# New place shifts, by operation name and by pair of heads, in the order of a fused attention, FFN and routed-expert kernel

## The chip, the cores and the metric

The kernel runs on one core of a Trainium2 chip. The time is device microseconds of one execution; the kernel before has a median of 493.71 us over three runs (492.6 to 497.37). The profile is of one further execution, with its own time.

## The reference, cut to what matters

Three layers are computed in a row on 1152 tokens (batch 2, sequence 576, model width 512 = 8 heads of 64): causal attention with a bias from a running sum, a dense feed-forward layer, and a layer of 8 experts of which each token takes one.

```python
# attention: q, k, v of 2 x 8 x 576 x 64
scores = scale * np.matmul(q, k.transpose(0, 1, 3, 2))
cum = np.cumsum(np.maximum(s, 0.0), axis=-1)
bias = -(cum[:, :, :, None] - cum[:, :, None, :])
scores = np.where(causal, -1000000000.0, scores + np.minimum(bias, 0.0))
attn = np.exp(scores - np.max(scores, axis=-1, keepdims=True))
attn = attn / (np.sum(attn, axis=-1, keepdims=True) + 1e-09)
x = np.matmul(attn, v)                      # to 1152 x 512
# dense layer: 512 -> 2048 -> 512
h = x @ w_in
x = (h * (1.0 / (1.0 + np.exp(-1.702 * h)))) @ w_out
# experts: argmax of 8 logits, at most 288 tokens each, 512 -> 1024 -> 512
expert_idx = np.argmax(x @ w_gate, axis=1)
y = np.maximum(disp @ w1, 0.0) @ w2         # disp: the tokens, gathered by expert
out[i] = gate_w[i] * y[expert_idx[i], pos[i]]
```

## The kernel before

**Attention** works on 8 pairs of heads, numbered 0 to 7. A pair has 5 row blocks t = 0 to 4 of 64, 128, 128, 128 and 128 rows. For one block, `unit` makes the scores on PE (L719, and the mask by L720) in the banks SC, takes the maximum on DVE (L741 or L745), the exponent on ACT (L750, tile pexp), casts it to 16 bits on DVE (L704, tile ph) and adds the low part on POOL (L764, L769). SP then issues a DMA transpose PT<-ph (L777; blocks 0 and 1 share the tile PT01, the others are PT2, PT3 and PT4). `av_unit` multiplies PT with the values V on PE (L797), scales on DVE (L809 to L812, tile xs) and transposes the result on PE (L821).

What a pair needs first: SP loads k and q (L667, tiles kraw and qraw, two of each), PE transposes them (L688), ACT or DVE copies them into the tile QK (L694, L697; QK0 and QK1 in turn), and SP adds two rows with the bias from a tensor cum_d in DRAM (L677, QK<-cum_d). The tensor cum_d is written once, at the start, by two DMAs (L542). Values are loaded by SP (L594, into spare tiles named vraw, th2, woL7 and wiL7 at the start) and split by ACT (L655) and DVE (L657) into V.

**The dense layer** loads its weights in pieces of 512 KB (L358, L361, tiles wraw0 to wraw2), converts them on ACT, DVE and POOL (L392 to L409) and multiplies in `mm1` (L433, L437) and `mm2` (L466, L467); part of this fills the gaps of the attention. **Routing** (about 335 to 347 us) computes logits, the ranks and the order of tokens; the first expert's tokens are gathered by PE (L1007 makes the selection on DVE, L1010 multiplies) and split into a high and a low part by `xs_first` (ACT L1306, L1312; DVE L1308, L1315). **Experts:** per expert `e_mm1` (L1372, L1374; DVE L1380 and L1384 behind it), `e_mm2` (L1401, L1403; DVE L1410) and stores; DVE also splits expert weights (L1295).

**What sets the order.** Every operation is put into the class `Plan` with a rank, its place. `Plan.run` makes a list schedule: on each engine, of the operations that it believes ready within 120 ns, the one with the lowest rank goes next. The instructions are then issued in that order; each engine runs its own in order, SP's DMA issues too. `SHIFT` is a table from a name to a number that is added to the rank. The name is made of the stage (a, b0 to b4 by row block, or c), the functions, the engine and the tile. So one number holds for, say, all transposes PT<-ph of row block 3 in all pairs.

Of the kernel before, what the change touches and what calls it, by code (L numbers as in the profile page):

```python
# [22 lines left out]
SHIFT = {  # L23
    "a.bias_keep.sp.cumd": 3.9, "a.bias_rows.sp.QKb": -7.7, "a.consts.a.pool.identF": -19.5, "a.consts.b.pool.": 13.3,
    "a.consts.dve.identB": -28.5, "a.consts.dve.ones1": 13.2, "a.consts.dve.ph": 22.6, "a.consts.dve.vss": 9.9,
    "a.consts.pool.QKb": 1.4, "a.consts.pool.V2o": 22.6, "a.prologue.dve.cum": 6.7, "a.prologue.dve.neg": 5.3,
    "a.prologue.dve.one": 16.1, "a.prologue.dve.one2": 25.2, "a.prologue.dve.s": 22, "a.prologue.sp.s": -32.6,
    "a.qk_T.act.QK": 9.4, "a.qk_T.dve.QK": -10.1, "a.qk_T.tr.pe.BK": 13.3, "a.qk_load.sp.raw": -15.6,
    "a.v_load.sp.vraw": 14.3, "a.v_scale.dve.gtb": 34.4, "a.v_scale.dve.scl": 37.3, "a.v_scale.pe.BK": 16.3,
# [1581 lines left out]
```

## Time and profile before

| | |
|---|---|
| median of 3 runs | 493.71 us |
| the profiled execution's own time | 495.86 us |
| its span in the trace | 494.1 us |
| PE busy | 465.5 us, 94% |
| DVE, ACT, POOL busy | 359.3, 328.6, 128.4 us |
| mean granted clock of PE | 0.979 |

The page gives the span in 40 slices of 12.35 us each, with the granted clock of TensorE in tenths; 1.0 is 2.4 GHz and 0.5 is 1.2 GHz. In a row of the timeline a bracket at the end gives how long the engine stood idle before the row and what the trace takes as the releaser. In a row of a table by stretches each engine has its busy time and, in brackets, its instructions.

### The profile page before, as it was taken

The numbers are of one execution on the slowest core, as the hardware profiler recorded it, in microseconds if no ns is written. First come the engines' busy times: TensorE is split into PE (matmuls) and PEld (weight loads), VectorE is DVE, ScalarE is ACT, GpSimd is POOL, SyncE is SP. The second block draws the span as 40 slices with busy tenths as digits, with TensorE's granted clock in tenths as the row PEclk, the third lists the DMA queues.
The fourth block names the chain that finished last, engine by engine and source line by source line (L and its number), as shares of the span: only waits on it lengthen the run. The fifth ranks groups of instructions, "written<-read, shape, count | busy, mean of one in ns | idle before, by whom it ended". The sixth has DMA issues, their size and how long they took to land.

```text
span 494.1 us, 9648 instructions
## 1 busy us (share of the span) xinstructions
PE 465.5 (94%) x3379; PEld 352.1 (71%) x3398; DVE 359.3 (73%) x817; ACT 328.6 (67%) x754; POOL 128.4 (26%) x136
## 2 busy tenths in 40 slices
PE   6599989999999999999999999999999999989993
PEld 5366666667677666766766966759688898878981
DVE  8867767888979988982324466846986879799980
ACT  3567878987557656673335346842886988899981
POOL 5616765867212222211000130002000110220250
PEclk9968989999999999999999999999999999999998
DMA  7997999978972554692000248821694687876820
GB/s 164 255 226 150 239 233 171 211 148 152 206 217 96 172 155 148 215 356 87 1 1 0 87 172 312 323 84 44 195 348 151 184 265 243 288 241 226 273 84 21
DMA packets 99047, 88.20 MB, mean 179 GB/s; under 512 B 66679, under 2 KB 77943, under 8 KB 98982
## 3 DMA queue, kind: packets, MB, share of 16 engines
q1 hardware_dynamic: 97108, 82.04, 61.3%
q0 software_dynamic: 1888, 5.52, 2.9%
q8 instruction: 27, 0.44, 0.4%
q14 instruction: 24, 0.20, 0.1%
HBM read 60.60 MB, written 14.19 MB: 151 GB/s over the span
## 4 chain that ended last, share of the span: by engine, by line
PE 49%; DMA 13%; DVE 12%; issue 10%; ACT 8%; POOL 5%; SPq 1%; POOLq 0%; DVEq 0%; ACTq 0%
PE SC L466 8%; PE SC L719 6%; PE MI L433 5%; DMA PT<-ph 5%; PE MX L433 4%; DMA out_dram<-x2R,small 4%; PE SC L467 3%; PE MI L437 2%; PE AV L1401 2%; PE AV L797 2%; PE MX L437 2%; DMA wraw<-in_moe_w_out_dram 2%; POOL ph L769 2%; PE MI L1372 2%; POOL ph L764 2%
## 5 line engine op out<-in xcount | busy, mean ns | idle before, releaser
L466 PE MATMUL SC<-woH,gtH 128*128 128x512 f32 x212 | 75.8, 481 | 0.0
L719 PE MATMUL SC<-QK 128*128 128x512 f32 (+4 forms) x192 | 65.1, 449 | 8.5 <-POOL ph L769 4.3
L447 DVE SCALAR_TENSOR_TENSOR gtH<-th,gtH 128x384 fp32r<-128x384 f32 x46 | 25.8, 561 | 40.0 <-ACT gtH L445 39.3
L764 POOL TENSOR_TENSOR ph<-pexp,ph 128x512 f16<-128x512 f32 (+4 forms) x32 | 44.7, 1398 | 31.8 <-DVE ph L704 26.3
L450 ACT ACTIVATE gtB<-th 128x384 bf16<-128x384 f32 x46 | 24.0, 521 | 37.1 <-PE SC L467 24.5
L433 PE MATMUL MI<-xT,wiH 128*128 128x384 f32 x216 | 47.0, 356 | 0.5 <-DVE th L443 0.4
L750 ACT ACTIVATE pexp<-SC,smA 128x192 f32<-128x192 f32 (+4 forms) x80 | 38.4, 520 | 12.7 <-DVE smA L741 9.2
L719 PEld LDWEIGHTS SC<-QK 128*128 128x128 f32 (+1 forms) x192 | 29.8, 197 | 23.1 <-issue 11.4
L466 PEld LDWEIGHTS SC<-woH,gtH 128*128 128x128 f32 x212 | 40.3, 194 | 3.2
L1295 DVE TENSOR_TENSOR wiL<-wraw,wiH 128x1024 bf16<-128x1024 f32 x32 | 38.9, 1221 | 3.7 <-ACT wiH L1294 3.5
L1295 DVE TENSOR_TENSOR woL<-wraw,woH 128x1024 bf16<-128x1024 f32 x32 | 38.9, 1218 | 3.1 <-ACT woH L1294 3.0
L1437 POOL DMA_INDIRECT out_dram<-x2R,small x8 | 9.9, 1240 | 119.1 <-ACT x2R L1464 82.5
L409 POOL TENSOR_TENSOR wiL<-wvi,wiH 128x512 bf16<-128x512 f32 x16 | 22.2, 1386 | 68.6 <-ACT wiH L405 64.2
L467 PEld LDWEIGHTS <-gtB 128*128 128x128 bf16 x138 | 13.2, 96 | 37.5 <-issue 37.2
L433 PEld LDWEIGHTS MI<-xT,wiH 128*128 128x128 f32 x216 | 37.8, 189 | 2.2 <-DVE th L443 0.9
L1118 POOL DMA_INDIRECT xs_d<-x2R,small x9 | 9.0, 996 | 112.9 <-DVE small L1058 57.3
L433 PE MATMUL MX<-xT,wiH 128*128 128x384 f32 x168 | 36.6, 358 | 0.1
L467 PE MATMUL SC<-woL,gtB 128*128 128x512 bf16 x94 | 36.7, 390 | 0.0
L1294 ACT ACTIVATE wiH<-wraw 128x1024 fp32r<-128x1024 f32 x32 | 33.6, 1055 | 1.9 <-DMA wraw<-in_moe_w_dram 1.4
L694 ACT ACTIVATE QK<-MI 64x288 f32<-64x288 f32 x57 | 24.1, 423 | 14.6 <-PE MI L688 9.0
L1294 ACT ACTIVATE woH<-wraw 128x1024 fp32r<-128x1024 f32 x32 | 33.5, 1055 | 0.4 <-DMA wraw<-in_moe_w_dram 0.4
L433 PEld LDWEIGHTS MX<-xT,wiH 128*128 128x128 f32 x168 | 29.6, 189 | 1.6 <-DVE th L443 0.8
(290 smaller groups left out, 1146.3 us busy)
## 6 DMA issues: line engine op xcount, KB each, us to landing
wraw<-in_moe_w_dram SPq DMA_DIRECT2D x64, 512.0 KB
wraw<-in_moe_w_in_dram SPq DMA_DIRECT2D x16, 512.0 KB
wraw<-in_moe_w_out_dram SPq DMA_DIRECT2D x16, 512.0 KB
xs_d<-x2R SPq DMA_DIRECT2D x16, 257.0 KB
kraw<-in_k_dram SPq DMA_DIRECT2D x8, 288.0 KB
qraw<-in_q_dram SPq DMA_DIRECT2D x8, 288.0 KB
out_dram<-x2R SPq DMA_DIRECT2D x9, 256.0 KB
x2R<-xs_d SPq DMA_DIRECT2D x8, 257.0 KB
```

What stands on the lines that cost most here:

```text
L409: e_.tensor_tensor(out=dlo, in0=vi.bitcast(F32), in1=dhi.bitcast(F32), op=ALU.subtract)
L433: nc.tensor.matmul(ps, lhsT=whi[:, kc], rhs=xT[:, a, kc, cs], start=(kc == 0 and a == 0), stop=False)
L447: pl.op("dve", t_dve(CN), lambda: nc.vector.scalar_tensor_tensor(out=gh[:, 1], in0=th, scalar=0.5, in1=gh[:, 0].bitcast(F32), op0=ALU.mult ...
L450: pl.op("act", t_act(CN), lambda: nc.scalar.activation(out=gb, in_=th, func=AF.Copy, scale=0.5), r=[("th", n % 2)], w=[("gtb", gi)] + xw)
L466: nc.tensor.matmul(o, lhsT=gh[:, a, ts], rhs=whi, start=(fc == 0 and a == 0), stop=False)
L467: nc.tensor.matmul(o, lhsT=gb[:, ts], rhs=wlo, start=False, stop=(fc == NFC - 1))
L694: pl.op("act", t_act(3 * TQ, False) + 130, lambda o=o, in_=in_, sc=sc: nc.scalar.activation(out=o, in_=in_, func=AF.Copy, scale=sc), r=[bk ...
L719: nc.tensor.matmul(o[:rows, j0:j1], lhsT=t_[:, 2 * r, i0:i0 + rows], rhs=t_[:, 2 * r + 1, j0:j1], start=True, stop=False)
L750: pl.op("act", t_act(wdt, False, 1), lambda o=o, r=r, nm=nm: nc.scalar.activation(out=pe[:rows, r, :wdt], in_=o[:rows, :wdt], func=AF.Exp, ...
L764: pl.op(eng, (t_pool if eng == "pool" else t_dve)(n * T_), lambda rs_=rs_, e_=e_: e_.tensor_tensor(out=hl[:, rs_, 0:T_], in0=pe[:rows, rs_ ...
L1294: pl.op("act", t_act(1024), lambda: nc.scalar.activation(out=dhi, in_=raw, func=AF.Copy), r=[rk], w=kh, rank=rank, after=after)
L1295: pl.op("dve", t_dve(1024), lambda: nc.vector.tensor_tensor(out=dlo, in0=raw, in1=dhi.bitcast(F32), op=ALU.subtract), r=[rk, ks[0], ks[2]] ...
```

## The change

All numbers of the table are new, and there are about 320 entries for about 205. Beside an entry for a name there may now be a second one for the name and a group: `@` in stage a, `@n` for the pair n of heads in stage b (`@x` behind the attention), `@n` for the n-th dozen of ranks in stage c. The operations themselves, 860 up to the order of tokens and 1773 in all that follows or overlaps, are the same.

```diff
 SHIFT = {
-    "a.bias_keep.sp.cumd": 3.9, "a.bias_rows.sp.QKb": -7.7, "a.consts.a.pool.identF": -19.5, ...
...
-        rank += SHIFT.get(self.name(eng, fn, w, rank), 0.0)
+        name = self.name(eng, fn, w, rank)
+        rank += SHIFT.get(name, 0.0) + SHIFT.get(name + self.group(name, rank), 0.0)
...
+    def group(self, name, rank):
+
+        return {"a": "@", "b": f"@{int(rank // 5)}" if rank < 40.0 else "@x", "c": f"@{int(rank // 12)}"}[name[0]]
```

The lines of the changed kernel are higher by 37 below the table (L677 is L714 there, L777 is L814).

**First place: the start, SP.** SP's issues from the V loads into spare tiles to the first transposes, before:

```order
L594 DMA th2_88<-in_v_dram 128x8x64
L594 DMA woL7_85<-in_v_dram 128x8x64
L594 DMA wiL7_81<-in_v_dram 128x8x64
L667 DMA kraw1_116<-in_k_dram 96x2x384
L667 DMA qraw1_114<-in_q_dram 96x2x384
L542 DMA cum_d_72<-QK1_112 8x2x1152 x2
L667 DMA kraw0_115<-in_k_dram 96x2x384
L667 DMA qraw0_113<-in_q_dram 96x2x384
L358 DMA wraw0_91<-in_moe_w_in_dram 128x4x256
L777 DMA_TRANSPOSE PT01_123<-ph01_122 128x8x128
L358 DMA wraw2_93<-in_moe_w_in_dram 128x4x256
```

The next issue there is `L677 DMA QK1_112<-cum_d_72`. The same stretch of the changed kernel, from the first write of cum_d on:

```order
L579 DMA cum_d_72<-QK1_112 8x2x1152 x2
L631 DMA th2_88<-in_v_dram 128x8x64
L631 DMA woL7_85<-in_v_dram 128x8x64
L631 DMA wiL7_81<-in_v_dram 128x8x64
L704 DMA kraw1_116<-in_k_dram 96x2x384
L704 DMA qraw1_114<-in_q_dram 96x2x384
L714 DMA QK1_112<-cum_d_72 2x2304
L395 DMA wraw0_91<-in_moe_w_in_dram 128x4x256
L395 DMA wraw2_93<-in_moe_w_in_dram 128x4x256
L814 DMA_TRANSPOSE PT01_123<-ph01_122 128x8x128
L704 DMA kraw0_115<-in_k_dram 96x2x384
```

The writes of cum_d went ahead of three V loads, and QK1<-cum_d went ahead of the two weight loads, the transpose PT01 and the loads of pair 2 (kraw0, qraw0). PT01 now stands behind wraw2.

On PE, in the kernel before, the rows around the first matmuls on QK1 with what each waits for (DMAHW4 is the semaphore of the transfer QK1<-cum_d there):

```order
L688 MATMUL MI_109<-identF_60,qraw1_114 128x96 [waits DMAHW4_49,Activation_49]
L688 MATMUL MI_109<-identF_60,qraw1_114 128x96 x2
L719 MATMUL SC1_106<-QK1_112 128x192 [waits DMAHW4_49,Activation_49,Pool_49]
L688 MATMUL MI_109<-identF_60,qraw1_114 128x96 x3
L719 MATMUL SC0_105<-QK1_112 64x64
L719 MATMUL SC1_106<-QK1_112 128x192 [waits Activation_49]
```

In the changed kernel the block of 64 rows goes first here, and its first matmul has the same kind of waits.

**Second place: pair 2, SP.** The issues between the transposes PT2 and PT4 of pair 2, before:

```order
L777 DMA_TRANSPOSE PT2_127<-ph2_124 128x10x128
L667 DMA qraw1_114<-in_q_dram 96x2x384
L594 DMA th2_88<-in_v_dram 128x8x64
L667 DMA kraw0_115<-in_k_dram 96x2x384
L677 DMA QK0_111<-cum_d_72 2x2304
L777 DMA_TRANSPOSE PT3_128<-ph3_125 128x14x128
L594 DMA woL7_85<-in_v_dram 128x8x64
L777 DMA_TRANSPOSE PT4_129<-ph4_126 128x18x128
```

And in the changed kernel:

```order
L814 DMA_TRANSPOSE PT2_127<-ph2_124 128x10x128
L631 DMA th2_88<-in_v_dram 128x8x64
L814 DMA_TRANSPOSE PT3_128<-ph3_125 128x14x128
L631 DMA woL7_85<-in_v_dram 128x8x64
L704 DMA qraw1_114<-in_q_dram 96x2x384
L714 DMA QK0_111<-cum_d_72 2x2304
L704 DMA kraw0_115<-in_k_dram 96x2x384
L814 DMA_TRANSPOSE PT4_129<-ph4_126 128x18x128
```

PT3 passed the loads of q and k and the bias rows; PT4 still stands behind them all.

**Third place: the end of routing, DVE.** The rows around `xs_first` (gtH is the high part of the first expert's tokens in four pieces, srt, sqr and ordi belong to the order of tokens), before:

```order
L1164 TENSOR_TENSOR sqr<-srt,iota_66 128x64
L1308 TENSOR_TENSOR gtH<-MI,gtH 128x224
L1165 TENSOR_TENSOR sqr<-sqr,iota_66 128x64
L1166 TENSOR_REDUCE srt_1961<-sqr 128x8
L1308 TENSOR_TENSOR gtH<-MX,gtH 128x224
L1308 TENSOR_TENSOR gtH<-SC_105,gtH 128x224
L1315 CAST gtB<-gtH 128x224
L1167 CAST ordi<-srt_1961 128x8
L1172 TENSOR_TENSOR sqr<-iota_66,srt 128x64
L1308 TENSOR_TENSOR gtH<-SC_105,gtH 128x224
```

And in the changed kernel:

```order
L1202 TENSOR_TENSOR sqr<-sqr,iota_66 128x64
L1203 TENSOR_REDUCE srt_1961<-sqr 128x8
L1345 TENSOR_TENSOR gtH<-MI,gtH 128x224
L1204 CAST ordi<-srt_1961 128x8
L1209 TENSOR_TENSOR sqr<-iota_66,srt 128x64
L1345 TENSOR_TENSOR gtH<-MX,gtH 128x224
L1345 TENSOR_TENSOR gtH<-SC_105,gtH 128x224
L1352 CAST gtB<-gtH 128x224
L1210 TENSOR_TENSOR sqr<-sqr,misc 128x64
L1211 TENSOR_REDUCE misc<-sqr 128x8
L1345 TENSOR_TENSOR gtH<-SC_105,gtH 128x224
```

Four small operations of the token order moved ahead of a piece of gtH that they stood behind: two ahead of the first piece (L1202, L1203) and two ahead of the last (L1210, L1211).

## Rows read from the trace of the kernel before

**Rows 1.** The page: span, PE's busy time, PE's granted clock in slices

```profile
span 494.1 us, 9648 instructions
PE 465.5 (94%) x3379; PEld 352.1 (71%) x3398; DVE 359.3 (73%) x817; ACT 328.6 (67%) x754; POOL 128.4 (26%) x136
PEclk9968989999999999999999999999999999999998
```

**Rows 2.** Table by stretches: length, busy us, granted clock, DMA share, GB/s

```profile
12.35:24.70 12.35, 6.88 (x36) 3.78 (x34) 10.87 (x23) 7.08 (x14) 8.60 (x8) 0.92 1.12 255
24.70:37.00 12.30, 11.96 (x90) 8.18 (x91) 7.90 (x16) 7.91 (x19) 2.29 (x3) 0.67 1.09 227
37.00:49.40 12.40, 11.77 (x111) 8.48 (x110) 9.34 (x21) 9.92 (x24) 7.73 (x9) 0.86 0.77 150
61.80:74.10 12.30, 10.19 (x114) 7.57 (x113) 8.24 (x18) 9.25 (x23) 7.80 (x7) 0.86 1.20 234
148.00:345.00 197.00, 196.50 (x1057) 141.09 (x1071) 125.26 (x302) 105.13 (x204) 25.10 (x21) 1.00 0.42 142
```

**Rows 3.** Timeline of PE, 11 to 35 us: start, duration, operation, idle before

```profile
11.61 0.81 PE L719 MATMUL SC<-QK 128*128 128x320 f32 x2 [0.92 <-ACT pexp L750]
...
24.68 0.98 PE L719 MATMUL SC<-QK 128*128 128x192 f32 x2 [4.32 <-POOL ph L769]
...
29.36 0.97 PE L797 MATMUL AV<-V,PT 128*128 128x65 f16 x14
30.14 1.41 PE L719 MATMUL SC<-QK 128*128 128x320 f32 x2
...
34.26 0.94 PE L719 MATMUL SC<-QK 128*128 128x448 f32 x2
```

**Rows 4.** Timeline of SP at 16 us: the issue of the bias rows

```profile
16.66 1.68 SPq L677 DMA_DIRECT2D QK<-cum_d  x1
```

**Rows 5.** The page's list of DMA issues: sizes of two kinds of load

```profile
wraw<-in_moe_w_in_dram SPq DMA_DIRECT2D x16, 512.0 KB
kraw<-in_k_dram SPq DMA_DIRECT2D x8, 288.0 KB
```

**Rows 6.** Timelines of ACT, POOL and DVE, 20 to 29 us

```profile
20.50 0.85 ACT L694 ACTIVATE QK<-MI 64x288 f32<-64x288 f32 x2
21.48 2.23 POOL L764 TENSOR_TENSOR ph<-pexp,ph 128x1024 f16<-128x1024 f32 x1 [1.11 <-DVE ph L704]
21.94 2.32 DVE L399 SCALAR_TENSOR_TENSOR wvi<-wvi,wraw 128x512 int32<-128x512 int32 x1 [0.20 <-ACT wvi L392]
27.76 0.75 DVE L657 SCALAR_TENSOR_TENSOR V<-vraw,misc,V 128x512 f16<-128x512 f32 x1 [2.07 <-ACT V L655]
```

**Rows 7.** Timelines of POOL, SP and PE around PT3 and PT4, 55 to 71 us

```profile
55.87 0.42 POOL L769 TENSOR_TENSOR ph<-pexp,ph 128x128 f16<-128x128 f32 x1
58.94 2.80 SPq L777 DMA_TRANSPOSE PT<-ph  x1
64.64 0.84 PE L797 MATMUL AV<-V,PT 128*128 128x65 f16 x22 [0.96 <-DMA PT<-ph]
69.89 1.26 PE L797 MATMUL AV<-V,PT 128*128 128x65 f16 x28 [1.07 <-DMA PT<-ph]
```

**Rows 8.** Timeline of PE at the end of attention

```profile
133.07 0.64 PE L821 MATMUL MX<-identF,xs 64*128 64x64 f32 x3 [0.70 <-DVE xs L812]
```

**Rows 9.** Timelines of DVE and PE at the first expert, 346 to 348 us

```profile
346.17 0.21 DVE L1165 TENSOR_TENSOR sqr<-sqr,iota 128x64 f32<-128x64 f32 x1
347.82 0.39 DVE L1308 TENSOR_TENSOR gtH<-SC,gtH 128x224 fp32r<-128x224 f32 x1
347.27 1.46 PE L1372 MATMUL MI<-gtH,wiH 128*128 128x448 f32 x4 [0.69 <-ACT gtB L1312]
```

**Rows 10.** Timelines of DVE and PE in an expert, 433 to 436 us

```profile
433.92 1.22 DVE L1295 TENSOR_TENSOR woL<-wraw,woH 128x1024 bf16<-128x1024 f32 x1
435.44 0.44 PE L1415 MATMUL SC<-identF,x2Tt 128*128 128x128 f32 x2 [0.94 <-DVE x2Tt L1410]
```

More of the change, by code (lines that the diff above doesn't have):

```diff
@@ L23 @@
 SHIFT = {
[L24 to L28, printed above, removed]
@@ L29 @@
-    "a.v_load.sp.vraw": 14.3, "a.v_scale.dve.gtb": 34.4, "a.v_scale.dve.scl": 37.3, "a.v_scale.pe.BK": 16.3,
[3 rows of a table removed]
-    "b.w_conv.low.dve.wraw": -28.8, "b.w_conv.main.act.wo": -6.4, "b.w_conv.rest.dve.wo": -25.6,
-    "b.w_conv.rest.pool.wo": 9.4, "b.w_conv.sign.dve.wvi": -7.6, "b.w_conv.top.act.wvi": 21.5,
[38 rows of a table removed]
-    "c.evac.dve.x2r": -1.4, "c.expert.ld.sp.eid": -39.6, "c.first_early.dve.sel": 28.3, "c.first_early.mm.pe.BK": 3.6,
-    "c.first_load.load.sp.x2r": 2.4, "c.first_rows.dve.sel": 7.1, "c.first_rows.pe.BK": -23.5, "c.keep.pool.": 14.7,
@@ L75 @@
-    "c.keep.sp.": 12.5, "c.logits.act.x2T": 10.4, "c.logits.dve.ix": -4.3, "c.logits.dve.lg": 9.3,
-    "c.logits.dve.mx": 23.7, "c.logits.dve.x2T": -33.3, "c.logits.mm.pe.BK": -39.3, "c.logits.pe.BK": -21.9,
-    "c.mm1.act.gt": 9.5, "c.mm1.act.gtb": -5.4, "c.mm1.act.th": 25.2, "c.mm1.dve.gtl": -9.1, "c.mm1.dve.th": 6.7,
-    "c.mm1.pe.BK": -24.6, "c.mm2.mm.pe.BK": -17.6, "c.order.dve.base0": -4.2, "c.order.dve.ov": 13.3,
-    "c.order.dve.srt": 31.1, "c.pool.iotaW": 16.2, "c.route.act.w8": 9.2, "c.route.count.pe.BK": -31.8,
@@ L80 @@
-    "c.route.dve.cnt": 26.7, "c.route.dve.gate": -28.3, "c.route.dve.idx": -23.8, "c.route.dve.oc": -5.1,
-    "c.route.dve.oh": 11.4, "c.route.dve.pos": 17.9, "c.route.dve.rel": -28.6, "c.route.dve.sb": -20.2,
-    "c.route.dve.se": 0.4, "c.route.dve.slot": -28.1, "c.route.dve.t3": 35.2, "c.route.dve.tok": -21.3,
-    "c.route.dve.w8": -37.5, "c.route.scatter.pool.xs": -26.9, "c.send.scatter.pool.": -8.7,
-    "c.w_conv.both.dve.wvi": -25.3, "c.w_conv.low.dve.wraw": -5.6, "c.w_conv.main.act.wi": 18.5,
@@ L85 @@
-    "c.w_conv.main.act.wo": 10.2, "c.w_conv.rest.dve.wo": 14.8, "c.w_conv.rest.pool.wi": -11.5,
-    "c.w_conv.sign.dve.wvi": 20.1, "c.w_conv.top.act.wvi": 29.1, "c.w_load.load.sp.wraw": 22.9,
-    "c.w_unit.act.wi": 18.2, "c.w_unit.act.wo": 22.4, "c.w_unit.dve.wi": 7.8, "c.w_unit.dve.wo": 6.2,
-    "c.w_unit.load.sp.wraw": -0.7, "c.xs_first.act.xsT": -14.6, "c.xs_first.act.xsTb": -2.9,
-    "c.xs_first.dve.xsTb": 19.9, "c.xs_first.dve.xsTl": -0.3, "c.xs_first.load.sp.meta": -23.2,
-    "c.xs_in.act.xsT": -21.8, "c.xs_in.act.xsTb": 21.1, "c.xs_in.dve.meta": -18.5, "c.xs_in.dve.xsTl": 9.8,
@@ L91 @@
-    "c.xs_in.load.sp.x2r": -38.7, "c.xs_in.tr.pe.BK": -1.5, "c.zero.pool.zrow": -8.2, "c.zeros.sp.out0": -1.9,
-    "c.zeros.sp.xs0": 2.5,
+    "a.bias_keep.sp.cumd": -12.8, "a.bias_rows.sp.QKb": -20.7, "a.consts.a.pool.identF": -19.6,
+    "a.consts.b.pool.": -18.8, "a.consts.dve.identB": -14.7, "a.consts.dve.ones1": 15.5, "a.consts.dve.ph": -8.2,
+    "a.consts.dve.vss": 2, "a.consts.pool.QKb": -14.5, "a.consts.pool.V2o": 10, "a.prologue.dve.cum": 5,
+    "a.prologue.dve.neg": 23.8, "a.prologue.dve.one": -10.1, "a.prologue.dve.one2": -22.4, "a.prologue.dve.s": -17.3,
@@ new lines @@
+    "a.prologue.sp.s": -5.9, "a.qk_T.act.QK": 23.2, "a.qk_T.dve.QK": 12.6, "a.qk_T.tr.pe.BK": -23.6,
+    "a.qk_load.sp.raw": 5.5, "a.v_load.sp.vraw": 14.9, "a.v_scale.dve.gtb": 33.3, "a.v_scale.dve.scl": -9.7,
[3 rows of a table added]
+    "b.w_conv.both.dve.wvi": -11.3, "b.w_conv.both.dve.wvi@x": -7.1, "b.w_conv.low.dve.wraw": 15,
+    "b.w_conv.low.dve.wraw@x": -8.6, "b.w_conv.main.act.wo": -10.8, "b.w_conv.rest.dve.wo": 1.2,
+    "b.w_conv.rest.pool.wo": 26, "b.w_conv.sign.dve.wvi": 20.9, "b.w_conv.top.act.wvi": -16.5,
@@ new lines @@
+    "b.w_load.load.sp.wraw": -22.2, "b.w_load.load.sp.wraw@x": -14.7, "b0.copy.act.ph": 35.3,
[58 rows of a table added]
+    "c.first_early.dve.sel": -19.7, "c.first_early.mm.pe.BK": 15.8, "c.first_load.load.sp.x2r": 13.8,
+    "c.first_load.load.sp.x2r@3": -17.8, "c.first_rows.dve.sel": 7.7, "c.first_rows.pe.BK": 4.8, "c.keep.pool.": 30.4,
[9 rows of a table added]
+    "c.route.dve.gate": 20.1, "c.route.dve.idx": 40, "c.route.dve.oc": -21.8, "c.route.dve.oh": 22,
+    "c.route.dve.pos": 10.3, "c.route.dve.rel": 3, "c.route.dve.sb": 13.1, "c.route.dve.se": -17.4,
@@ new lines @@
+    "c.route.dve.slot": -31.8, "c.route.dve.t3": 23, "c.route.dve.t3@3": 12.9, "c.route.dve.tok": -19.9,
+    "c.route.dve.w8": -7.4, "c.route.scatter.pool.xs": 2, "c.send.scatter.pool.": -13, "c.w_conv.both.dve.wvi": -1.7,
+    "c.w_conv.both.dve.wvi@0": 12.1, "c.w_conv.low.dve.wraw": 14.3, "c.w_conv.low.dve.wraw@0": 24.3,
+    "c.w_conv.main.act.wi": -0.9, "c.w_conv.main.act.wo": -5.6, "c.w_conv.rest.dve.wo": 10.1,
+    "c.w_conv.rest.dve.wo@0": 15.3, "c.w_conv.rest.pool.wi": 17.8, "c.w_conv.sign.dve.wvi": 34.3,
[6 rows of a table added]
@@ new lines @@
+    "c.w_unit.load.sp.wraw@7": -21.4, "c.xs_first.act.xsT": -9.7, "c.xs_first.act.xsTb": 29.5,
+    "c.xs_first.dve.xsTb": 2.7, "c.xs_first.dve.xsTl": -10.8, "c.xs_first.load.sp.meta": 0.2, "c.xs_in.act.xsT": 12.2,
+    "c.xs_in.act.xsT@9": 11, "c.xs_in.act.xsTb": -7.1, "c.xs_in.dve.meta": 33.7, "c.xs_in.dve.xsTl": 10.2,
+    "c.xs_in.dve.xsTl@11": 33.6, "c.xs_in.dve.xsTl@9": 21.9, "c.xs_in.load.sp.x2r": -16.9,
+    "c.xs_in.load.sp.x2r@5": -15.5, "c.xs_in.tr.pe.BK": -19.7, "c.xs_in.tr.pe.BK@5": -13.1, "c.xs_in.tr.pe.BK@8": 5.5,
@@ L93 @@
+    "c.zero.pool.zrow": -14, "c.zeros.sp.out0": -7.4, "c.zeros.sp.xs0": 2.6,
 }
```

117 rows, old and new, of the table SHIFT are left out of this document.

## The prediction

> **What bounds the kernel now.** I read the page first, for PE's share. PE is busy for 465.5 of 494.1 us, and from 148 to 345 us it is busy for 196.50 of 197.00 [rows 1, 2]. An order that leaves the work as it is can give nothing in that stretch; it can give only what PE stands idle, and what it loses at half clock. So I looked next at the table by stretches and at the clock line. The idle time lies mostly ahead of 148 us, and below full clock are the slices from about 20 to 49 us, one at about 62 to 74 us, and the tail [rows 1, 2]. Then I followed PE's timeline for its idle gaps, and for each the engine or queue that ended it. The largest is 4.32 us, ahead of the first matmul on QK1 at 24.68 us [rows 3]; then 1.07 and 0.96 us for transposes PT<-ph of pair 2 [rows 7], 0.70 us at the end of attention [rows 8], and 0.69 us at the first expert [rows 9]. Last I compared the order of SP, DVE and PE at these places, before and now.
>
> **Part 1, the start.** The trace puts the 4.32 us down to POOL's L769, but POOL writes nothing that this matmul reads. The order says what it waits for: the transfer QK1<-cum_d, ACT and POOL. POOL's part of QK1 is a fill from the kernel's first microseconds. ACT's copy ends at 20.50 + 0.85 = 21.35 [rows 6]. What is left is the transfer, issued at 16.66 [rows 4] behind a queue of loads, so it landed shortly ahead of 24.68.
>
> Now it stands ahead of two weight loads of 512 KB, the loads of k and q of pair 2 (288 KB each) and PT01 [rows 5]. At the 255 GB/s of that stretch [rows 2], these loads alone are 1.64 MB / 255 GB/s = 6.4 us, so the transfer lands at about 24.5 - 6.4 = 18.1 or sooner. Its source is written sooner too: the writes of cum_d passed three V loads. PE then waits for ACT alone, until 21.35, and the wait shrinks from 4.32 to about 1.1: at most 3.3 us.
>
> What is late next? The first product with V, at 29.36 before [rows 3], needs the second piece of V from DVE. Before, it was done at 27.76 + 0.75 = 28.51, because ACT's half stood behind copies that themselves waited for PE [rows 6]. In the changed kernel ACT makes it ahead of these copies, and DVE makes it right after the weight conversion: L399 ends at 21.94 + 2.32 = 24.26 [rows 6], then L402 and two L657. Taking 0.75 for each of the three [rows 6], that ends at 24.26 + 2.25 = 26.5. L399 took 2.32 us beside a long POOL operation, L764 [rows 6]; both stand beside each other still, so I keep this length. PE reaches the product with V at 26.5 in place of 29.36: **-2.9**. Both ends: 0 if something else there is late (rival B), -3.3 by the first wait alone, and more if the clock comes back earlier (rival A). PT3 of this pair now passes the next pair's loads too, so it doesn't eat the gain at 32.7; PT4 stands behind four issues that it led before, and I take no gain there beyond what is carried on.
>
> **Part 2, pair 2.** POOL had ph3 ready at 55.87 + 0.42 = 56.29, but SP issued PT3 only at 58.94, behind loads of q, V and k and the bias rows, and PE waited 0.96 for it and then 1.07 for PT4 [rows 7]. Now PT3 follows PT2 and one V load, so it can go about 2 us earlier; the 0.96 goes. PT4 stands behind the same loads as before, and its 1.07 may only grow by what PE is early. The lower end is 0, since PE arrives earlier by the 0.96 and waits that much more for PT4; the upper is 0.96 + 1.07 = 2.0, if PT4 moves along by the 2 us. SP's issues ahead of PT4 are then all early, so I take the middle: **-1.0**.
>
> **Part 3, end of attention.** The transposes L821 that waited 0.70 [rows 8] now stand behind two products with V, which cover DVE's xs: **-0.5**, between 0 and -0.7.
>
> **Part 4, routing.** Four operations of the token order now stand ahead of pieces of gtH on DVE, at about 0.21 each [rows 9]; two more stand ahead of the selection L1007. The last piece ended at 347.82 + 0.39 = 348.2 before, and e_mm1 waited 0.69 already [rows 9]. Nothing covers this: PE has nothing else there. Three to four of 0.21 on the path: **+0.7**, between 0 and 6 x 0.21 = 1.3.
>
> **Part 5, the clock.** The granted clock is 0.86 in 37 to 49 and 0.86 in 62 to 74 [rows 2]. Between the levels 2.4 and 1.2 GHz, 0.86 means 0.28 of 12.3 us = 3.4 us at the lower one in each. How much that costs is seen in one pair of matmuls of equal shape: 0.81 at full, 1.41 at half clock [rows 3]. A stretch of 3.4 us so costs up to 1.7, less where PE would only have waited. I expect that one dip goes or shrinks, as PE idles less ahead of it: **-0.9**, half of one, between 0 and -3.4.
>
> The Trainium skill, "TensorE: Matmul & The Clock Gate", Part 1, says that the low clock is the default and activity releases it. By that rule both dips are after-effects of the waits and would go with them. The trace agrees that they follow idle stretches, and the sum by it would be rival A's.
>
> **Parts at nothing.** The dense layer from 148 to 345 us has 0.5 us of idle time in all [rows 2], and its weight loads come early enough to hide being moved. The load of the first expert's rows that were already sorted (L984) moved behind three weight loads on SP, but PE reads it only right ahead of the gather. In the experts the order of e_mm1 and e_mm2 is shuffled; there is little idle time to win, and what it may cost is rival C.
>
> **The sum.** -2.9 - 1.0 - 0.5 + 0.7 - 0.9 = -4.6 on the profiled execution's 495.86, so 491.3. That execution is 2.15 above the median of 493.71 (its span is 494.1 [rows 1]; 1.8 lie around it and stay). So I forecast 491.3 - 2.15 = **489.1**, some 0.9% less.
>
> **The rivals.**
> A, larger: the clock comes back with the waits. The half-speed stretch of 24.7 to 37 us (0.67, so 0.66 x 12.3 = 8 us [rows 2]) goes too. Two score blocks there would take 0.81 for 1.41 each, another 1.2; both dips 3.4, PT3 and PT4 2.0. Sum -2.9 - 1.2 - 3.4 - 2.0 - 0.6 + 0.7 = -9.4: **484.3**. Against it: PE was busy in those stretches also because other engines set its pace.
>
> B, the change doesn't do what it seems to: the queue only changes who is late. DMA is full from 12 to 37 us [rows 2], so what one transfer gains others lose: PT01 now stands behind one more load of 512 KB, 2.1 us at 255 GB/s, and QK1's gain is given back at the product with V, which reads PT01. In that case parts 1 and 5 fall away: -1.0 - 0.5 + 0.7 = -0.8, **492.9**. Against it: PT01's own source was ready early, and 29.36 leaves it room.
> The Trainium skill, "DMA: Bandwidth & Descriptors", section "Issuing engines are not separate DMA queues", says that all transfers run on the same 16 engines whoever starts them. It speaks for B, and the full share in the table agrees.
>
> C, slower: DVE in the experts. Where an e_mm1, e_mm2 or transpose stands right behind the step that feeds it, and a weight split L1295 of 1.22 us is ahead on DVE, PE waits as it did at 434.5 for 0.94 [rows 10]. In the changed order five e_mm1 come back to a bank after only one other, against two before, but only six after a little more, against thirteen. The mechanism eats the forecast's gain from 4.6 / 0.94 = 5 such waits on; with eight it is 489.1 + 7.5 = **496.6**, and over 1% slower it is from ten on. Against it: the closest pairs are only three more.
>
> **Chances.** Forecast 0.50 (its own range 487 to 491.5), A 0.17, B 0.23, C 0.10. About 1% is what a measurement of this kernel can tell from no change: 488.8 and 498.6. The forecast lies close to the first, and I give it 0.22 of its 0.50 below; with A that makes 0.39, and with small gains that I left out (first units, 0.92 at 10.70 us [rows 3]) 0.42. Slower than 498.6 needs ten waits: 0.06. The rest is 0.52. The range reaches into A and over B: 484.5 to 495.
>
> **What would show it.** Part 1: PE's wait ahead of the first matmul on QK1 under 1.5 us, ended by ACT, and the product with V at about 26.5. Part 2: PT3 of pair 2 issued within 1 us of the POOL row, and no wait for it. Part 3: no wait of L821 near 130 us. Part 4: the first e_mm1's wait at 1.2 to 1.6. Part 5: one clock dip less between 37 and 74 us. It would be wrong if a new wait of over 2 us stands between 20 and 75 us, or if DVE makes PE wait more than 4 us longer in the experts.

## The result

The changed kernel takes 490.4 us in the median of 20 runs (486.28 to 497.17), the kernel before 494.32 us in the median of as many (491.76 to 500.02). The ratio is 0.9914, with a 95% interval of 0.9894 to 0.9934: 4.3 us less, within 3.3 to 5.2. The ratio, here and below, leaves out runs in a slower state of the chip (4 of the 20 of the changed kernel), so it gives 4.3 us where the two medians differ by 3.9. The forecast was 489.1 us and 4.6 us less, so the sum was right. Its parts were not: most of them lie in attention, and most of the gain lies in the experts.

The profiled execution of the changed kernel spans 490.1 us against 494.1 [rows 1], which is 4.0 us less. The page of the changed kernel:

```profile
span 490.1 us, 9708 instructions
PE 464.5 (95%) x3378; PEld 352.8 (72%) x3398; DVE 359.0 (73%) x817; ACT 328.0 (67%) x754; POOL 126.0 (26%) x136
PEclk9987989989999999999999999999999999999998
```

PE's work is the same within a microsecond, and its clock line has one dip more than in [rows 1], not one less. The table by stretches of the changed kernel (as [rows 2], with one stretch more at 98.8):

```profile
12.35:24.70 12.35, 8.40 (x43) 4.82 (x43) 11.57 (x25) 9.59 (x19) 8.79 (x8) 0.91 1.17 249
24.70:37.00 12.30, 11.95 (x120) 8.31 (x120) 10.66 (x22) 8.64 (x21) 4.94 (x6) 0.81 1.25 259
37.00:49.40 12.40, 10.57 (x73) 7.53 (x72) 6.48 (x14) 7.75 (x20) 6.18 (x7) 0.72 1.01 199
61.80:74.10 12.30, 10.53 (x122) 7.77 (x122) 7.21 (x17) 8.70 (x22) 6.69 (x7) 0.86 1.13 201
98.80:111.20 12.40, 11.76 (x102) 8.64 (x103) 8.53 (x20) 9.37 (x23) 5.90 (x7) 0.86 0.68 133
148.00:345.00 197.00, 196.93 (x1065) 142.56 (x1080) 127.37 (x307) 105.89 (x206) 26.75 (x21) 1.00 0.43 141
```

From 24.7 to 37 us the clock is better than before (0.81 for 0.67), from 37 to 49.4 worse (0.72 for 0.86), and there PE is also idle for 12.40 - 10.57 = 1.8 us, where it was idle for 0.6. In this execution, what the start gave is gone again a few microseconds later. PE's timeline of the changed kernel at the start (as [rows 3]):

```profile
21.20 0.30 PE L756 MATMUL SC<-QK 128*64 128x64 f32 x2 [1.09 <-POOL ph L806]
...
25.80 0.97 PE L834 MATMUL AV<-V,PT 128*128 128x65 f16 x14
...
40.01 0.94 PE L834 MATMUL AV<-V,PT 128*128 128x65 f16 x14 [1.83 <-DMA PT<-ph]
```

The wait ahead of QK1 is 1.09 us, and the first product with V starts at 25.80 in place of 29.36. At 40.01 the first product of pair 1 has waited 1.83 for its transpose.

Two marks divide the span. The first e_mm1 starts at 346.79, against 347.27 [rows 9], only 0.5 us sooner. From there to PE's last instruction it is 134.97 us (to 481.76), against 138.43 (to 485.70). So 3.5 of the 4.0 us lie in the experts in these two executions. What PE waited for there, before (the releasers of its waits from 347.27 us on: us in total, times, longest):

```profile
PE SC L1415 <- DVE x2Tt L1410: 1.2, 2, 0.9
PE MI L1372 <- ACT gtB L1312: 0.7, 1, 0.7
PE SC L1345 <- ACT gtB L1354: 0.6, 1, 0.6
PE MI L1372 <- DVE wvi L1380: 0.3, 1, 0.3
PE MI L1374 <- DVE woL L1295: 0.2, 1, 0.2
```

And in the changed kernel, from 346.79 us on:

```profile
PE MI L1409 <- ACT gtB L1349: 0.7, 1, 0.7
PE MI L1409 <- DVE wvi L1417: 0.2, 1, 0.2
PE MI L1409 <- DVE gtH L1345: 0.2, 1, 0.2
```

The table by stretches has the same in two rows. Before, from the first e_mm1 to 475 us:

```profile
347.27:475.00 127.73, 125.21 (x1017) 109.20 (x1018) 108.40 (x242) 111.05 (x286) 16.83 (x12) 1.00 0.73 238
```

And in the changed kernel:

```profile
346.79:475.00 128.21, 127.72 (x1050) 112.20 (x1051) 111.59 (x248) 112.24 (x296) 15.97 (x12) 1.00 0.72 237
```

PE is idle for 127.73 - 125.21 = 2.5 us before and for 0.5 after. The 0.7 us in the waits are the first e_mm1's own in both. All waits behind it but 0.4 us are gone: those for DVE's x2Tt (the result of e_mm2 that PE transposes next, as in [rows 10]) and for ACT's gtB.

### The profile page after: what moved, and what is told of

Its sections match the earlier page's. It is cut to its first block, busy times and chain, and to the rows that moved or that the text cites. A ratio compares the mean times of both kernels' runs of the same rounds, so it can differ in the third digit from the quotient of the medians.

```text
span 490.1 us, 9708 instructions
## 1 busy us (share of the span) xinstructions
PE 464.5 (95%) x3378; PEld 352.8 (72%) x3398; DVE 359.0 (73%) x817; ACT 328.0 (67%) x754; POOL 126.0 (26%) x136
## 4 chain that ended last, share of the span: by engine, by line
PE 74%; DVE 7%; DMA 6%; issue 4%; POOL 3%; ACT 3%; SPq 1%; POOLq 0%; ACTq 0%
PE SC L503 11%; PE MI L470 7%; PE AV L1438 7%; PE MX L470 6%; DMA PT<-ph 5%; PE SC L756 5%; PE SC L504 5%; PE MI L1409 4%; PE MI L474 3%; PE MX L1409 3%; PE AV L503 3%; PE AV L1440 3%; PE MX L474 3%; PE AV L834 3%; POOL ph L801 2%
## 5 line engine op out<-in xcount | busy, mean ns | idle before, releaser
L756 PE MATMUL SC<-QK 128*128 128x512 f32 (+4 forms) x192 | 66.5, 454 | 6.0 <-ACT pexp L787 1.9
L470 PE MATMUL MI<-xT,wiH 128*128 128x384 f32 x216 | 48.6, 361 | 0.0
L787 ACT ACTIVATE pexp<-SC,smA 64x64 f32<-64x64 f32 (+4 forms) x80 | 38.2, 520 | 14.6 <-DVE smA L778 12.3
L446 POOL TENSOR_TENSOR wiL<-wvi,wiH 128x512 bf16<-128x512 f32 x16 | 23.7, 1480 | 56.7 <-ACT wiH L442 52.8
L480 DVE SCALAR_TENSOR_TENSOR th<-th,MI 128x384 f32<-128x384 f32 x27 | 14.8, 548 | 29.8 <-ACT th L478 29.8
L478 ACT ACTIVATE th<-MI 128x384 f32<-128x384 f32 x27 | 13.1, 486 | 32.2 <-PE MI L474 31.6
```

The source lines that it names most:

```text
L470: nc.tensor.matmul(ps, lhsT=whi[:, kc], rhs=xT[:, a, kc, cs], start=(kc == 0 and a == 0), stop=False)
L756: nc.tensor.matmul(o[:rows, j0:j1], lhsT=t_[:, 2 * r, i0:i0 + rows], rhs=t_[:, 2 * r + 1, j0:j1], start=True, stop=False)
L787: pl.op("act", t_act(wdt, False, 1), lambda o=o, r=r, nm=nm: nc.scalar.activation(out=pe[:rows, r, :wdt], in_=o[:rows, :wdt], func=AF.Exp, ...
```

## The experiments

Two theories stood after the result. Theory 1: the gain is all in the experts, and what attention wins at the start it gives back. Theory 2: attention carries its gain, as predicted. Each run below is timed beside the kernel before on the same chip. In the table, the stretch to the first e_mm1 is attention, dense layer and routing; the next column is from there to PE's last instruction. Both are from one profiled execution each, the ratio is from the timed ones.

| kernel | ratio to before (95%) | first e_mm1 at | to PE's end |
|---|---|---|---|
| before | 1 | 347.27 | 138.43 |
| changed | 0.9914 (0.9894 to 0.9934) | 346.79 | 134.97 |
| stage a alone | 1.0136 (1.0093 to 1.0179) | 352.99 | 138.41 |
| stage c alone | 0.9946 (0.9911 to 0.9980) | 344.48 | 135.97 |
| stages a, b | 1.0018 (0.9991 to 1.0045) | 347.41 | 138.86 |
| stages a, c | 1.0068 (1.0044 to 1.0092) | 349.18 | 136.27 |
| stages b, c | 1.0499 (1.0469 to 1.0529) | 373.08 | 136.06 |
| bias rows moved | 1.0022 (0.9997 to 1.0047) | 345.85 | 139.11 |
| swap of weight loads | 0.9956 (0.9931 to 0.9981) | 347.38 | 135.15 |
| transposes first | 0.9988 (0.9964 to 1.0013) | 347.70 | 135.40 |
| weight units of c alone | 1.0111 (1.0080 to 1.0142) | 346.75 | 143.70 |
| steps of c alone | 1.0287 (1.0254 to 1.0321) | 344.78 | 151.96 |
| quarter loads | 0.9876 (0.9841 to 0.9911) | 345.03 | 135.14 |
| last loads behind the transposes | 0.9888 (0.9864 to 0.9912) | 347.33 | 134.98 |

How far can the two columns be trusted? The kernel with the steps of c alone, taken up below, and the kernel before have the same order on SP, ACT, DVE and POOL up to 335 us, and yet their first e_mm1 starts at 344.78 and 347.27. With quarter loads the order on SP, ACT and DVE is that of the changed kernel, and it starts at 345.03 for 346.79. So differences of up to 2.5 us in the column of the first e_mm1 are the spread of single executions. Worked out as in the prediction, PE's time at the low clock from 12.35 to 150 us is 6.9 us for 17.0 in the first pair and 13.8 for 20.8 in the second: the earlier one has less of it in both. Which of the two causes the other isn't shown. The last column is steadier: 138.4 to 139.1 us in the four kernels with the old order in the experts, 135.0 to 136.3 in the eight with the new one.

**The stages apart.** Five kernels take the new shifts of some stages and the old ones of the others (the table is written out in them; OLD and NEW stand for the two tables here, and KEEP is "a", "c", "ab", "ac" or "bc"):

```diff
-SHIFT = NEW
+SHIFT = {**{k: v for k, v in OLD.items() if k[0] not in KEEP},
+         **{k: v for k, v in NEW.items() if k[0] in KEEP}}
```

Stage a alone:

> Only the shifts of stage a (constants, prologue, bias rows, first loads) are those of the changed kernel; stages b and c keep the old table. Theory 1 (the gain at the start is given back): the wait ahead of the first matmul on QK1 falls from 4.32 to about 1.1 us and PE is 2.5 to 3.5 us ahead at 30 us, but is back within 1 us of the kernel before by 150 us, since the transposes PT<-ph then end the waits; time within 1.5 us of the kernel before. Theory 2 (the gain is carried on, as the prediction had it): PE is still 2 us or more ahead at 150 us, time 2 to 3.5 us less.

Stage c alone:

> Only the shifts of stage c (rest of the dense layer, routing, experts) are those of the changed kernel. Theory 1 (the whole gain of the change lies in the experts): from the first e_mm1 to PE's last instruction 138.4 us become about 135, time 3 to 4 us less than before. Theory 2 (the gain comes from attention, experts as before): first e_mm1 to last unchanged within 0.7 us, time 0 to 1 us more, by the routing operations that moved ahead on DVE.

Stages a and b:

> The shifts of stages a and b (all of attention) are those of the changed kernel, stage c keeps the old table. Theory 1: attention as in the changed kernel, which was 0.5 us ahead at the first expert; time 0 to 1 us less than before. Theory 2 (attention carries the gain): 3 to 4 us less.

Stages a and c:

> Stages a and c new, stage b (order within attention) old. Theory 1: as stage c alone, 3 to 4 us less than before, and what stage a alone gives on top (0 to 1.5). If the new order within attention is what gives the start's gain back, this is 2 to 3 us faster than the changed kernel; if the transposes give it back in any order, it is within 1 us of it.

Stages b and c:

> The shifts of stages b and c new, stage a old. Stage a alone cost 7 us and with stage b it cost 2. Theory 1 (a and b belong together: b's order of the bias rows needs a's early write of cum_d): the write of cum_d is late again, the wait ahead of the first matmul on QK1 is 2 us or more, and the time is 1 to 4 us above the changed kernel. Theory 2 (a only costs): 1 to 3 us below the changed kernel.

The experts behave as theory 1 says: with the old stage c the last column is 138.4 to 138.9, with the new one 136.0 to 136.3, and 135.0 in the changed kernel. Stages a and b together show no gain (1.0018, with 0.9991 to 1.0045), and stage c alone gives 0.5% (2.7 us, within 1.0 to 4.4), where theory 1 had 3 to 4 us. The changed kernel gains more than these two together, 0.9% against about 0.4%; the intervals overlap, and whether that rest is real stays open. About 1 us of it stands in the last column: the five kernels of the table with all new shifts, the changed one included, take 135.0 to 135.4 us there, the three without stage a or b 136.0 to 136.3. SP, ACT, DVE and PE go through the experts in the same order in all eight, so what makes this 1 us isn't shown.

In attention neither theory foresaw what happens when its two stages are parted. Stage a alone makes the kernel 1.4% slower, stages a and c 0.7%, stages b and c without a 5.0%: none of the three times is in the range of either theory. The first has the old wait still, at 22.08 us (PE's timeline of that kernel):

```profile
26.03 0.98 PE L723 MATMUL SC<-QK 128*128 128x192 f32 x2 [3.95 <-POOL ph L773]
```

It sends cum_d early, but QK1<-cum_d has its place from stage b and stays back, so the wait stays too. What the rest of its 1.4% comes from isn't shown. The waits of stages b and c in its first 170 us (releasers of PE's waits):

```profile
PE SC L756 <- ACT pexp L787: 7.3, 13, 1.5
PE AV L834 <- DMA PT<-ph: 7.1, 5, 2.8
PE MI L725 <- ACT QK L731: 4.8, 4, 3.2
PE MX L858 <- DVE xs L849: 4.1, 3, 2.5
```

These are waits of PE for ACT, DVE and the transposes, many of them, and no single one. The wait of 2 us or more ahead of the first matmul on QK1, that theory 1 names, isn't among them; there it is the first product with V that waits 2.82 us for its transpose. The granted clock from 0 to 148 us is 0.87 as well, against 0.93 in the changed kernel. The new order of stage b is good only together with the new start.

**The bias rows alone.** The order of the kernel before, with three of SP's issues moved after the schedule is made (numbers are those of operations):

```diff
+MOVES = [(27, "after", 20), (28, "after", 27), (90, "before", 69)]
...
+        if n0 == 0:
+            for m, side, t in MOVES:
+                order.remove(m)
+                order.insert(order.index(t) + (side == "after"), m)
         free["dma"] = dma_free
```

> The kernel before with three DMA issues moved on SP's queue and nothing else: the two writes of cum_d ahead of the three V loads, and QK1<-cum_d ahead of the first weight load and PT01. Theory 1 (the wait ahead of the first matmul on QK1 is that transfer): the wait falls from 4.32 us (2.4 in another profile of the same order) to 1.1 to 1.4, ended by ACT; PE is 1 to 3 us ahead at 30 us; of this some is left at 150 us and the time is 0 to 2.5 us less. Theory 2 (the wait is POOL's, as the trace's releaser says): it stays at 2.4 or more, time unchanged within 1 us.

The wait is 1.10 us (timelines of ACT and PE, this kernel), so the transfer was its cause, not POOL. What ends it now is ACT's copy, done at 21.50 + 0.86 = 22.36:

```profile
21.50 0.86 ACT L703 ACTIVATE QK<-MI 64x288 f32<-64x288 f32 x2
```

```profile
22.45 0.56 PE L728 MATMUL SC<-QK 128*128 128x192 f32 x2 [1.10 <-issue]
```

PE is 2.2 us ahead of the kernel before at the score block that starts at 24.7 there. Yet the timed runs are no faster: 1.0022 (0.9997 to 1.0047). A part of the reason is in the profiles of three other kernels here, whose order is that of the kernel before up to far behind this place. It is the same wait in each (stage c alone, the weight units alone, the steps alone):

```profile
23.33 0.65 PE L740 MATMUL SC<-QK 128*128 128x192 f32 x2 [2.40 <-DMA QK<-cum_d]
```

```profile
23.12 0.56 PE L727 MATMUL SC<-QK 128*128 128x192 f32 x2 [1.81 <-DMA QK<-cum_d]
```

```profile
24.31 0.98 PE L730 MATMUL SC<-QK 128*128 128x192 f32 x2 [2.72 <-DMA QK<-cum_d]
```

The trace itself names the transfer in these. And it is 1.8 to 2.7 us, not 4.32: the profile that the prediction was made from had this wait at nearly twice its usual length, in an execution 1.5 us above the median of 20. What there is to win by the move is 0.7 to 1.6 us, and not 3.2. The timing leaves no room for that either, since the interval ends at 0.15 us less. Where it is lost again isn't shown; that the first e_mm1 starts 1.4 us sooner in the profile is within the spread named above.

**Where the start's lead goes in the changed kernel.** ACT waits there for a weight load, and DVE at the same time (timeline of ACT, the changed kernel):

```profile
38.65 0.68 ACT L429 ACTIVATE wvi<-wraw 128x512 f32<-128x512 f32 x1 [1.38 <-DMA wraw<-in_moe_w_in_dram]
```

It is wraw1, that the change moved from ahead of PT2 of pair 0 to ahead of PT01 of pair 1. The next kernel swaps it with a load that is needed later:

```diff
+MOVES = [(70, "before", 156), (156, "after", 235)]
```

> The changed kernel with two weight loads of 512 KB swapped on SP's queue and the second of them later: wraw1, that ACT and DVE waited for at 38.65 us, goes where the second wraw0 stood, and that one goes behind PT4 of pair 1. Theory 1 (the start's gain is given back by wraw1, which the change had moved from ahead of PT2 to ahead of pair 1's PT01): the wait of 1.83 us at 38.17 falls below 0.6, the waits of ACT and DVE for wraw vanish, the low clock from 39 to 46 us goes; PE is 2 us or more further at 60 us; time 1.5 to 4 us less than the changed kernel. Theory 2 (PT01 is late by itself, the queue is full whatever the order): the wait stays above 1.2 us and the time is within 1 us of the changed kernel.

ACT's wait for the load is gone, but PE's for the transpose stays (PE's timeline of this kernel):

```profile
40.17 0.94 PE L843 MATMUL AV<-V,PT 128*128 128x65 f16 x14 [1.47 <-DMA PT<-ph]
```

That is 1.47 where theory 1 wanted under 0.6, and the time is no less (0.9956 against 0.9914, some 2 us more, where theory 2 had 1 at most).

How much of the 1.83 belongs to the order, and how much to one execution? The kernel with stages a and b has the changed kernel's order on every engine up to 145 us (PE's timeline):

```profile
40.33 0.59 PE L818 MATMUL AV<-V,PT 128*128 128x65 f16 x14 [0.84 <-DMA PT<-ph]
...
67.59 1.30 PE L818 MATMUL AV<-V,PT 128*128 128x65 f16 x28 [3.17 <-DMA PT<-ph]
```

Here the same wait is 0.84, no low clock follows it (1.00 from 37 to 49.4 us, for 0.72), and at the score block of 49.62 us PE is still 3.3 us ahead of the kernel before, which starts it at 52.88. The lead then goes into the wait for PT4 of pair 2, 3.17 for 1.75. In the kernel with the last loads behind the transposes, of the same order up to 120 us, the first wait is 2.12. So the lead is given back at transposes in both executions, but at which one is a draw, and one profile of a kernel that moves one load can't tell much about one wait. The next kernel adds the other transposes:

```diff
+MOVES = [(70, "before", 156), (156, "after", 235), (407, "after", 323), (376, "after", 407), (494, "after", 376),
+         (561, "after", 539), (637, "after", 561), (824, "after", 765), (831, "after", 824), (838, "after", 793)]
```

> The swap of the run before, and three more moves on SP's queue of the changed kernel: q, bias rows and k of later pairs behind PT4 of pair 2; the weight load and the bias rows of pair 7 behind PT01 of pair 5; two weight loads behind the second half of PT3 of the last pair and one behind PT4. Theory 1 (each remaining wait of attention is a transpose behind loads that are not urgent): the waits of 1.75 at 66.95, 0.91 at 98.53 and 1.50 at 134.96 fall below 0.6 each; the first expert starts 4 to 8 us earlier than in the changed kernel and the time is 484 to 487. Theory 2 (what is moved back is late next): the waits for PT<-ph are replaced by waits of PE for MI<-qraw, kraw or QK, and the time is within 1.5 us of the swap alone.

The wait of 1.75 for PT4 of pair 2 is gone, and others stand in its place (PE's timeline of this kernel, three places):

```profile
57.51 1.02 PE L765 MATMUL SC<-QK 128*128 128x448 f32 x2 [2.23 <-ACT pexp L796]
...
68.28 0.30 PE L765 MATMUL SC<-QK 128*64 128x64 f32 x2 [2.18 <-DMA QK<-cum_d]
...
102.94 1.05 PE L843 MATMUL AV<-V,PT 128*128 128x65 f16 x16 [2.60 <-DMA PT<-ph]
```

The second of them is the bias rows that had been moved behind PT4: theory 2, what is moved back is late next. The third is a transpose again. The time is 1.6 us above the swap alone by the ratios (0.9988 and 0.9956), with intervals that overlap. One part did as wanted: from 110 to 150 us PE was busy for 39.69 of 40 us. So that part was run alone:

```diff
+MOVES = [(824, "after", 765), (831, "after", 824), (838, "after", 793)]
```

> The changed kernel with three weight loads on SP's queue moved behind the last pair's transposes, two behind the second half of PT3 and one behind PT4, and nothing else. In the kernel with all moves PE idled 0.31 us from 110 to 150, against 1.83 in the changed kernel. Theory 1 (that part is worth it by itself): the wait of 1.50 at 134.96 is under 0.6 and the time 1 to 2 us less than the changed kernel, about 489. Theory 2: the weights are then late for the dense layer, a wait appears after 140 us, time unchanged within 1 us.

Its stretch from 110 to 150 us, in the table by stretches:

```profile
110.00:150.00 40.00, 39.70 (x363) 28.02 (x362) 34.94 (x72) 26.24 (x56) 16.59 (x21) 1.00 0.82 192
```

The wait of 1.50 is gone and no other takes its place there. In this execution, the slowest of the six timed, the first e_mm1 still is no earlier (347.33 for 346.79). The median is 489.27 us and the ratio 0.9888 (0.9864 to 0.9912), against 0.9914 (0.9894 to 0.9934) for the changed kernel. It is the fastest of the kernels that leave no work out, but the intervals overlap, so that it beats the changed kernel isn't shown.

**Are the DMA engines the limit?** The changed kernel with smaller weight loads during attention:

```diff
+def CUT(n):
+    return 1 if n < 9 else 4
...
-                dq.dma_start(out=raw.rearrange("p (k f) -> p k f", k=KC), ...
+                dq.dma_start(out=raw.rearrange("p (k f) -> p k f", k=KC)[:, :CUT(n)], ...
```

> The changed kernel, where the nine loads of dense weights during attention carry a quarter of their bytes (the rest of these weights is left at zero, so that the dense layer lacks it; POOL fills the three tiles once at the start). Theory 1 (attention is paced by the DMA engines, so that a transfer that goes earlier makes another late): the waits of PE for PT<-ph (6.0 us in the changed kernel) fall to 2 or less, and the first expert starts 4 us or more earlier than at 346.8. Theory 2 (the transposes are late for their sources or their own length on the queue): the waits stay above 4 us and the first expert starts within 2 us of 346.8.

The first rows of PE's waits in its first 150 us:

```profile
PE AV L840 <- DMA PT<-ph: 5.8, 4, 2.7
PE SC L762 <- ACT pexp L793: 1.8, 6, 0.5
```

The waits for PT<-ph are 5.8 us, as they were with all bytes (6.0 in the changed kernel, 5.7 with stages a and b). The first e_mm1 starts 1.8 us earlier, within the spread. By its own terms theory 2 has it. But the waits at 40 and 67 us are about those of the kernel with stages a and b, and the DMA engines are still full around the larger one (PE's timeline, and the table by stretches):

```profile
40.23 0.59 PE L840 MATMUL AV<-V,PT 128*128 128x65 f16 x14 [0.74 <-DMA PT<-ph]
...
67.07 1.01 PE L840 MATMUL AV<-V,PT 128*128 128x65 f16 x28 [2.70 <-DMA PT<-ph]
```

```profile
61.80:74.10 12.30, 9.60 (x72) 6.53 (x70) 6.20 (x14) 7.77 (x21) 6.03 (x6) 0.86 1.13 210
```

The edit takes some 3.5 MB out of the 29 MB that move in the first 148 us, and from 61.8 to 74.1 us the share is 1.13 as in the changed kernel. So the run speaks against the bytes of these nine loads as what PE waits for. That full engines pace the transposes it doesn't exclude, and whether it is that, their sources or their own length on SP's queue, no run parts.

**The experts' gain.** Two kernels take one part of stage c's shifts each, on the table before; FIRST is the list of name beginnings. (The new table has 376 entries and the old one 255, not about 320 and 205. Of the new ones 148 are of stage c, and the two parts have 18 and 45 of these; the rest, mostly of the dense layer and routing, stays old in both.)

```diff
-SHIFT = OLD
+SHIFT = {**OLD, **{k: v for k, v in NEW.items() if k.startswith(FIRST)}}
```

With FIRST = ("c.w_unit",):

> The kernel before, with only the new shifts of the experts' weight units (loads, ACT L1294 and DVE L1295 in the old lines). Theory 1 (the experts' gain is that the weight splits stand later on DVE and ACT, behind what PE waits for): the waits of PE for DVE in the experts (2.6 to 3.6 us of idle time from the first e_mm1 on) fall to about 1, the stretch from the first e_mm1 to PE's end is 135 to 136.5 us in place of 138.4 to 139.1. Theory 2 (it is the order of PE's own steps): 138 or more.

With FIRST = ("c.e_", "c.xs_in"):

> The kernel before, with only the new shifts of the experts' own steps (e_mm1, e_mm2, xs_in, the rows out, on all engines) and the old ones for the weight units. Theory 2 (PE's own order puts more work between a step and what reads it): first e_mm1 to PE's end 135 to 136.5 us. Theory 1 (the weight splits' places): 138 or more. If both kernels give half each, the two parts work apart; if neither does, they belong together.

Neither part gives the gain, and each alone is much worse than nothing: 143.70 and 151.96 us from the first e_mm1 to PE's end, for 138.43. PE's waits from there on, with the weight units' shifts alone:

```profile
PE SC L1423 <- DVE x2Tt L1418: 3.2, 4, 1.3
PE MI L1380 <- DVE wvi L1388: 2.6, 3, 1.3
```

And with those of the steps alone:

```profile
PE MI L1383 <- DVE wvi L1391: 4.0, 6, 1.1
PE SC L1426 <- DVE x2Tt L1421: 2.5, 3, 1.5
PE AV L1412 <- DVE x2Tt L1421: 2.4, 1, 2.4
```

These are the waits of rival C: PE stands for DVE at e_mm1 and at the transposes of e_mm2, and a weight split is ahead on DVE. One of them, with the weight units' shifts alone (timelines of DVE and PE):

```profile
400.89 1.22 DVE L1303 TENSOR_TENSOR woL<-wraw,woH 128x1024 bf16<-128x1024 f32 x1
402.09 0.35 DVE L1418 TENSOR_TENSOR x2Tt<-AV,x2R 128x200 f32<-128x200 f32 x1
```

```profile
402.50 0.44 PE L1423 MATMUL SC<-identF,x2Tt 128*128 128x128 f32 x2 [1.30 <-DVE x2Tt L1418]
```

They appear when one of the two parts is new and the other old, and all but 0.2 to 1.0 us of them are gone when all of stage c is new. So the two theories on the experts, weight splits or PE's steps, are both wrong as stated: it takes the two together. Whether it takes the rest of stage c's shifts too, no run parts.

## Why the prediction was right, and where not

**Part 1, the start** (-2.9). The mechanism held in all its steps. The wait fell to 1.09; the transfer was its cause, which the run that moves it alone shows; the product with V started at 25.80, where 26.5 was forecast, and PE was 3.6 us ahead of the profile before. Two things failed. The price was read from one execution: 4.32 there, 1.8 to 2.7 in three others of the same order, so the term was mis-sized at about twice and more. And "it doesn't eat the gain" failed: the lead of 3.4 us at 40 us is 0.7 at 54, by the wait of 1.83 at 38.17 and the low clock behind it. In another execution of the same order the lead held to 50 us and went at PT4 of pair 2; in neither was it carried on.

**Part 2, pair 2** (-1.0). PT3 was issued at 56.21, 0.9 us after its source, and its wait is gone, as forecast. The middle that I took for PT4 was wrong. The changed kernel's issue and what waited for it (timelines of SP and PE):

```profile
61.62 4.90 SPq L814 DMA_TRANSPOSE PT<-ph  x2
```

```profile
68.70 1.02 PE L834 MATMUL AV<-V,PT 128*128 128x65 f16 x28 [1.75 <-DMA PT<-ph]
```

PT4 now stands behind q, the bias rows and k, and its wait grew from 1.07 to 1.75. Of 2.03 us 1.75 are back: -0.3, near the end at 0, for the reason given there. With stages a and b, the same order, it is 3.17, so this part too is known to a microsecond or so at best. The prediction's own sign of being wrong, a new wait of over 2 us between 20 and 75 us, is absent from the changed kernel's profile and stands in that one.

**Part 3, end of attention** (-0.5). The wait of L821 shrank from 0.70 to 0.21, as forecast, but the product with V behind it, which I had not priced, waits 1.50 where it waited 0.48 (PE's timeline of the changed kernel):

```profile
134.32 0.64 PE L858 MATMUL MX<-identF,xs 64*128 64x64 f32 x3 [0.21 <-DVE xT L863]
136.46 0.83 PE L834 MATMUL AV<-V,PT 128*128 128x65 f16 x22 [1.50 <-DMA PT<-ph]
```

So this part is +0.5 in place of -0.5. Its cause is three weight loads on SP's queue among the last transposes: with them behind, the wait is gone in both kernels that move them, and with them in place it is 1.10 to 1.83 in the profiles with the changed kernel's order.

**Part 4, routing** (+0.7). The order was read rightly, and the price was wrong. DVE and PE in the changed kernel:

```profile
347.40 0.38 DVE L1345 TENSOR_TENSOR gtH<-SC,gtH 128x224 fp32r<-128x224 f32 x1
```

```profile
346.79 0.88 PE L1409 MATMUL MI<-gtH,wiH 128*128 128x448 f32 x3 [0.69 <-ACT gtB L1349]
347.84 0.47 PE L1409 MATMUL MI<-gtH,wiH 128*128 128x448 f32 x1 [0.17 <-DVE gtH L1345]
```

The first e_mm1 still waits for ACT's gtB, 0.69 as before [rows 9]; only its last matmul waits for DVE's last piece, 0.17. DVE had idle time between the pieces, and the small operations went into it. The end of the range at 0 was the right one.

**Part 5, the clock** (-0.9). No gain is seen. Worked out as in the prediction, from 12.35 us on, the time at the low level is 2.0 + 8.1 + 3.5 + 3.4 = 17 us before [rows 2] and 2.2 + 4.7 + 6.9 + 3.4 + 3.5 = 21 us after, since the dip at 43 became longer and one came at 101. But that is one execution each: others of the order before have 7 to 14 us, others of the order after 14 to 24. The mean granted clock of the timed runs is 0.981 after and 0.981 to 0.982 before, so on the whole the time at the low level neither fell nor rose. Its 1.7 us for a dip of 3.4 us is also a little more than the pair of matmuls named there gives, 3.4 x (1 - 0.81 / 1.41) = 1.4. The rule of the Trainium skill on which rival A rested ("TensorE: Matmul & The Clock Gate", Part 1: the low clock is the default, activity releases it) agrees with where the dips lie: behind the waits at 38, 67 and 98.5 us. Not every wait has a dip behind it, though: after the wait of 1.50 that ends at 136.46 the granted clock is 1.00 to 148 us.

**Parts at nothing.** This is the step that failed most: the experts' idle time was put at nothing. "In the experts [...] there is little idle time to win" was a judgement from the page's shares. The table by stretches would have given 2.5 us of idle time behind the first e_mm1. Of the gain of 3.5 us, 2.0 are that; the rest lies in time that the trace counts as busy, and what it is isn't shown. I priced a reordering there at nothing for want of a view, and gave it only a rival with the wrong sign.

So -4.6 came out as -4.3 by luck, by two errors that balance: the terms ahead of the first e_mm1, -4.6 together, came to -0.5 there, and the experts, priced at nothing, gave 3.5. The rival that the queue only changes who is late (B) describes attention best: it had -0.8, and stages a and b together measured between -0.4 and +2.2 (1.0018 with its interval). Its own reason, that the DMA engines are full, stays open: with quarter loads the waits are the same, but the engines are still full where the largest one stands. The rule of the Trainium skill beside it ("DMA: Bandwidth & Descriptors", "Issuing engines are not separate DMA queues") isn't tested by that. The rival of larger gain (A) fell, since the time at the low clock stayed and PT4 still made PE wait; its sum also has -0.6 for part 3, where the forecast has -0.5. The slower rival (C) is a real mechanism, as the two part tables show at 5 and 13 us, but the full table removes these waits.
